# Bank assignment and order in the front of an attention + two-MoE kernel, and the place of one batch's sums of v

## The chip, the cores and the metric

One core of a Trainium2 chip. The time is the device time of one execution, in microseconds, as the median of several runs; lower is better. Before the change it is 967.26 us (three runs, 966.04 to 967.92).

## What is computed

```python
def _attn_ref(q, k, v):                    # 4 batches, 8 heads, 576 tokens, 64 wide
    q_d, k_d, v_d = means over 4 tokens    # 144 down-sampled tokens
    out_up = np.repeat(sm_attn(q_d, k_d, v_d), 4, axis=2)
    scores = scale * np.matmul(q, k.transpose(0, 1, 3, 2))
    scores = np.where(abs(i - j) < 4, scores, -1e9)      # a band of 7
    return out_up + softmax(scores) @ v
...
    x = attn.reshape(2304, 512)            # tokens of all batches
    x = (silu(x @ w_gate) * (x @ w_val)) @ w_out         # 512 -> 1536 -> 512
    h = x @ w_in                                         # 512 -> 2048
    return (h * clip(h + 3, 0, 6) / 6) @ w_out2          # -> 512
```

The weights arrive as 64-bit floating-point numbers. All results are float32.

## The kernel before

**The main loop** (from L1050) goes through five blocks of 8, 6, 8, 8 and 6 groups of 64 tokens, at most 512 tokens each. A block has 68 units, 36 for the first MoE layer (kinds G, V and O) and 32 for the second (H and P); a unit is 12 matmuls (the last two O or P units of a block are done together). Both operands are split into a high and a low part, so three products stand for one. `prefetch(i)` (L240) loads the raw weights of unit i + 8 on SyncE's queue, and converts and splits those of nearer units on ScalarE and VectorE. Beside the units of a block, VectorE works on the banded attention of a later batch, and TensorE on its down-sampled attention (`down_main`, L850; one job a unit from unit 36 on).

**The front** (`first_batch`, L317) prepares batch 0 on TensorE, ahead of unit 0:
- `load_T` (L436) transposes q and k, two heads (one index c of four) at a time: for each half two filler matmuls that keep TensorE at work, three transposes, and an evacuation by VectorE (q) or ScalarE (k).
- `sums(c)` adds groups of four tokens; `down_scores(c)` (L473), `down_trans(c)` (L502) and `down_values(c)` (L513) are the down-sampled attention of two heads: scores, maximum, four exponentials; norm, transposes, copies; values. The values read `vd`, which `load_vd` (L366) loads in four pieces through two buffers and adds up on GpSimd.
- The banded attention runs over five tiles of 122 query tokens: `scores(i)` (L528; the band as a matmul, 16 products, two maxima, 8 exponentials), `norm(i)`, `trans(i)` (L580), `values(i)` (L594). Values add the down-sampled result and leave the two parts of x in `xr`.
- Unit 0 is done in two column halves, 244 and 268 wide (L33 `HALVES`), so that its first half needs tiles 0 and 1 alone.

**PSUM** has 8 banks by tag: mm (two), acc0 to acc3, pa, px. In the front, `load_T` goes around acc0, acc1 and acc2; `down_scores` uses mm; scores(i) use acc0 and acc1 for even tiles and mm for odd ones; trans use acc2 and acc3; `down_values` acc3; `down_trans` and `values` pa and px.

**What sets the order.** A compile-time scheduler orders each engine's instructions by readiness and program order, and each engine then runs its queue in that order. `keep_in_program_order` (in `together`, `fill`, `late` and `behind`) pins an instruction behind the one traced just before it on its engine. In the front the fills, the transposes of `load_T`, the scores, `down_scores` and `down_values` are pinned; the other transposes and `values` are not. The order of calls is written out by hand (L635 to L678).

**Sums of later batches.** `down_sums(b, ...)` (L279) is a generator: for each of four tokens in a group it issues two GpSimd DMAs (halves of 72 groups) for q and k, then for v, the later three adding to what lies in SBUF. Each `next` gives one operand's pair. For batch 1 the 12 steps are spread over the front; for batches 2 and 3 they go along with a block, behind a gate: a one-element GpSimd copy that reads the last block's output tile (L280 to L282).

Of the kernel before, what the change touches and what calls it, by code (L numbers as in the profile page):

```python
# [10 lines left out]
F32 = mybir.dt.float32  # L11
# [24 lines left out]

VAL0 = {1: 2}
EXP_AT = 26

EARLY = 6  # L40

# [4 lines left out]
def tile_kernel(  # L46
# [12 lines left out]
    nc = tc.nc  # L59

    B, H, S, D = q.shape
    DM = H * D
# [3 lines left out]
    NJ = S // 4  # L66
    NJH = NJ // 2
    W = 7
    NC = DM // P
# [7 lines left out]
    UMAX = max(BLOCKS)  # L77
# [10 lines left out]
    def bank(tag, name, bufs=1):  # L88
        return pp.tile([P, 512], F32, tag=tag, name=name, bufs=bufs)
# [186 lines left out]

    dn, qk = {}, {}

    def down_sums(b, dn, qk):  # L279
        if b > 1:  # L280
            done = state["os"]
            tc.keep_in_program_order(nc.gpsimd.tensor_copy(consts[:, 60:61], done[:, (UMAX // 2 - 2) * DM:][:, :1]))  # L282
        for ws in ("qk", "v"):
            for t in range(4):
                for w in ws:
                    if t == 0:
                        dn[w] = sp.tile([NJH, 2, H, D], F32, tag="dn" + w, name=f"dn{w}{b}", bufs=1)
                    src = {"q": q, "k": k, "v": v}[w]
                    for half in range(2):
                        tok = src[b, :, half * NJH * 4:(half + 1) * NJH * 4, :].rearrange("h (j t) d -> j t h d", t=4)  # L290
                        how = {"accum_op": ALU.add} if t else {}
                        tc.keep_in_program_order(nc.gpsimd.dma_start(dn[w][:, half], tok[:, t], **how))
                    yield
# [23 lines left out]
    def first_batch():  # L317
# [6 lines left out]
        with tc.tile_pool(name="fp", bufs=1) as fp:  # L324
# [111 lines left out]
            def load_T(w, c):  # L436
                src = qn[w, c // 2]
                for th in range(2):
                    tag = ("acc0", "acc1", "acc2")[turn[0] % 3]
                    turn[0] += 1  # L440
                    ps = bank(tag, f"fT{w}{c}{th}")
                    fill(ps, 2)
                    ps = ps[:, :S // 2]
                    for t in range(3):
                        tc.keep_in_program_order(nc.tensor.transpose(
                            ps[:, t * TT:(t + 1) * TT],
                            src[:, 3 * th + t, c % 2 * 2:c % 2 * 2 + 2].rearrange("j h d -> j (h d)"),
                            ident[:TT, :TT],
                        ))
                    if w == "q":  # L450
                        nc.vector.tensor_scalar(
                            qT[:, c, th * S // 2:(th + 1) * S // 2], ps, 0.125, None, op0=ALU.mult
                        )
                    else:
                        nc.scalar.activation(kT[:, c, 3 + th * S // 2:3 + (th + 1) * S // 2], ps, AF.Copy)

            def sums(c):

                nc.vector.tensor_reduce(
                    qs[:, c], qT[:, c].rearrange("p (j t) -> p j t", t=4), axis=AX.X, op=ALU.add  # L460
                )
                nc.scalar.activation(ds[:, c], qs[:, c], AF.Copy, scale=1 / 16)
                nc.vector.tensor_reduce(
                    dk[:, c], kT[:, c, 3:S + 3].rearrange("p (j t) -> p j t", t=4), axis=AX.X, op=ALU.add
                )
# [7 lines left out]
            def down_scores(c):  # L473

                pss = []
                for par in range(2):
                    ps = bank("mm", f"fdS{2 * c + par}", 2)
                    if par:
                        fill(ps, 1)
                    pss.append(ps[:NJH, :2 * NJ].rearrange("p (g j) -> p g j", g=2))  # L480
                for half in range(2):
                    for par in range(2):
                        rows = slice(par * D, par * D + D)
                        together(nc.tensor.matmul(
                            pss[par][:, half], ds[rows, c, half * NJH:(half + 1) * NJH], dk[rows, c, :],
                            start=True, stop=True,
                        ))
                nm = fp.tile([NJH, 2, 2], F32, tag="fdnm", name=f"fdnm{c}", bufs=4)
                pd = fp.tile([NJH, 2, 2, NJ], F32, tag="fdpd", name=f"fdpd{c}", bufs=4)
                sd = fp.tile([NJH, 2, 2], F32, tag="fdsd", name=f"fdsd{c}", bufs=4)  # L490
                for par in range(2):
                    nc.vector.tensor_reduce(nm[:, par], pss[par], axis=AX.X, op=ALU.max, negate=True)
                    for half in range(2):
                        nc.scalar.activation(
                            pd[:, par, half], pss[par][:, half], AF.Exp, bias=nm[:, par, half:half + 1],
                            accum_out=sd[:, par, half:half + 1],
                        )
                dst[c] = pd, sd
# [12 lines left out]
                    nc.scalar.activation(dpt[h], pt, AF.Copy)  # L511

            def down_values(c):  # L513
                po = bank("acc3", f"fdO{c}")[:, :NJ]
                for kh in range(2):
                    for par in range(2):
                        together(nc.tensor.matmul(
                            po[par * D:par * D + D], vd[:, kh, 2 * c + par, :], dpt[2 * c + par][:, kh, :],
                            start=kh == 0, stop=kh == 1,
                        ))  # L520
                nc.vector.tensor_copy(od[:, c], po)
# [110 lines left out]
                    put_cols(bi, t0 + a - starts[bi] * UT, xf[:, :, a:e])  # L632
                    a = e

            ahead = down_sums(1, dn, qk)  # L635
            for c in range(NC):
                load_T("q", c)
                load_T("k", c)
                if c == NC - 1:
                    scores(0)  # L640
                if c:
                    down_scores(c - 1)
                sums(c)
                if c == 2:
                    prefetch(3 - LR)
                if c >= 2:
                    down_trans(c - 2)
            down_values(0)
            down_scores(3)
            next(ahead)  # L650
            scores(1)
            prefetch(4 - LR)
            norm(0)
            down_trans(2)
            down_values(1)
            next(ahead)
            trans(0)
            down_trans(3)
            down_values(2)
            scores(2)  # L660
            prefetch(5 - LR)
            norm(1)
            down_values(3)
            values(0)
            for i in range(1, NT):
                next(ahead, None)
# [368 lines left out]
    for bi in range(NB):  # L1035
# [30 lines left out]
        if db:  # L1066
            sums = down_T(db, dn, qk)
            if bi:
                sums = chain(down_sums(db, dn, qk), sums)
        for i in range(bi * NU, (bi + 1) * NU):  # L1070
            m = i - bi * NU
            prefetch(i)
# [19 lines left out]
            next(main, None)  # L1092
            if m == NU - EARLY:
                load_ahead(at + 1)
            step_x(limit)
            next_tick()
        if bi + 1 < NB:
# [37 lines left out]
```

## Time and profile before

| | |
|---|---|
| median of 3 runs | 967.26 us |
| the profiled execution: device time, span | 962.81 us, 961.0 us |
| busy: TensorE, its weight loads | 934.2 us, 789.1 us |
| busy: VectorE, ScalarE, GpSimd | 733.5 us, 506.7 us, 111.0 us |
| mean granted TensorE clock | 0.990 of full speed |
| moved by DMA | 160.79 MB |

PE is TensorE's matmuls, PEld its weight loads, DVE VectorE, ACT ScalarE, POOL GpSimd, SP SyncE; a queue issuing DMAs has a q behind its name. Matmul ends are modelled, so neighbouring ones can overlap by some tenths of a microsecond. Tiles carry the program's names: fT is the bank of `load_T`, fdS, fdT and fdO those of `down_scores`, `down_trans` and `down_values`, fS, fPT and fO those of the five tiles' scores, transposes and values; held are the exponentials, turned the transposed ones, vd and fvd the pieces and sums of batch 0's v, dnq, dnk and dnv the sums of later batches, pO the down-sampled values of these.

### The profile page before, as it was taken

How to read it: one execution, taken by the hardware profiler on the slowest of the kernel's cores; microseconds unless marked ns; L12 is line 12 of the kernel's file. 1: busy time of each engine (PE TensorE's matmuls, PEld its weight loads, DVE VectorE, ACT ScalarE, POOL GpSimd, SP SyncE). 2: the span in 40 equal slices, each digit the busy share in tenths (PEclk: the TensorE clock that was granted, in tenths of full speed). 3: DMA queues.
4: the chain of work that ended last, by engine and by line, in shares of the span. 5: the costliest groups of instructions: out<-in, count | busy, mean ns of one | idle time of the engine just before them, and what ended most of it. 6: DMA issues, size and time to landing. Idle time of an engine off the chain costs nothing.

```text
span 961.0 us, 12930 instructions
## 1 busy us (share of the span) xinstructions
PE 934.2 (97%) x4800; PEld 789.1 (82%) x4800; DVE 733.5 (76%) x1067; ACT 506.7 (53%) x945; POOL 111.0 (12%) x115
## 2 busy tenths in 40 slices
PE   8779999999999999999999999999999999999997
PEld 5567888777799988878888778888888888999996
DVE  7689967799889979999664799996347994445652
ACT  4676667876554577543244764443335444444542
POOL 5742000000053300015410000000000000000000
PEclk9789999999999999999999999999999999999999
DMA  8999999466699823359962212462323223434331
GB/s 207 170 271 316 327 341 351 155 209 226 238 287 270 176 72 108 123 189 237 203 139 96 78 66 85 160 216 90 108 88 105 92 88 112 152 132 132 119 123 33
DMA packets 116339, 160.79 MB, mean 167 GB/s; under 512 B 61868, under 2 KB 83756, under 8 KB 116276
## 3 DMA queue, kind: packets, MB, share of 16 engines
q1 hardware_dynamic: 67892, 131.41, 42.3%
q0 software_dynamic: 43488, 10.72, 11.1%
q10 hardware_dynamic: 4896, 17.83, 4.7%
q8 instruction: 38, 0.62, 0.3%
q14 instruction: 25, 0.20, 0.1%
HBM read 137.29 MB, written 22.54 MB: 166 GB/s over the span
## 4 chain that ended last, share of the span: by engine, by line
PE 83%; DVE 11%; ACT 3%; issue 2%; DMA 1%; SPq 0%; ACTq 0%; DVEq 0%
PE pH L938 17%; PE aP L980 16%; PE pG L938 15%; PE aO L980 15%; PE pV L938 15%; DVE wr L237 2%; DVE pv L809 1%; ACT held L560 1%; PE pS L863 1%; DVE xf L838 1%; DVE h L954 1%; PE pO L713 1%; DMA k<-in_k_dram 1%; DVE pv L813 1%; PE pPT L706 1%
## 5 line engine op out<-in xcount | busy, mean ns | idle before, releaser
L237 DVE TENSOR_TENSOR wr<-w,wr 128x1024 fp32r<-128x1024 f32 x170 | 207.5, 1221 | 121.6 <-ACT wr L236 121.3
L236 ACT ACTIVATE wr<-w 128x1024 fp32r<-128x1024 f32 x170 | 179.7, 1057 | 132.4 <-issue 63.1
L938 PE MATMUL pH<-x,wr 128*128 128x512 f32 (+1 forms) x960 | 212.4, 372 | 0.0
L980 PE MATMUL aP<-wr,gH 128*128 128x512 f32 x864 | 211.4, 395 | 0.3 <-ACT gH L955 0.3
L938 PEld LDWEIGHTS pH<-x,wr 128*128 128x128 f32 x960 | 173.0, 188 | 25.1 <-issue 2.5
L980 PEld LDWEIGHTS aP<-wr,gH 128*128 128x128 f32 x864 | 159.6, 188 | 35.1 <-issue 2.7
L938 PE MATMUL pG<-xr,wr 128*128 128x512 f32 (+3 forms) x732 | 156.5, 368 | 3.8 <-ACT xr L273 3.2
L938 PE MATMUL pV<-xr,wr 128*128 128x512 f32 (+1 forms) x720 | 153.4, 368 | 0.0
L980 PE MATMUL aO<-gV,wr 128*128 128x512 f32 (+1 forms) x720 | 152.7, 368 | 0.0
L938 PEld LDWEIGHTS pG<-xr,wr 128*128 128x128 f32 x732 | 133.4, 190 | 21.4 <-ACT xr L273 3.8
L938 PEld LDWEIGHTS pV<-xr,wr 128*128 128x128 f32 x720 | 130.9, 188 | 16.7
L980 PEld LDWEIGHTS aO<-gV,wr 128*128 128x128 f32 x720 | 130.8, 188 | 16.7
L953 ACT ACTIVATE h<-pH,consts 128x512 f32<-128x512 f32 (+1 forms) x80 | 51.5, 644 | 59.7 <-PE pH L938 59.4
L944 ACT ACTIVATE sl<-pG 128x512 f32<-128x512 f32 (+1 forms) x60 | 33.3, 556 | 72.9 <-PE pG L938 72.8
L955 ACT ACTIVATE gV<-sl 128x512 fp32r<-128x512 f32 (+1 forms) x60 | 35.0, 583 | 65.6 <-DVE sl L950 65.5
L955 ACT ACTIVATE gH<-h 128x512 fp32r<-128x512 f32 (+1 forms) x80 | 46.9, 586 | 32.1 <-DVE h L954 31.8
L954 DVE SCALAR_TENSOR_TENSOR h<-h,pH 128x512 f32<-128x512 f32 (+1 forms) x80 | 50.5, 631 | 14.8 <-ACT h L953 14.2
L772 DVE TENSOR_TENSOR pr<-q,k 128x1792 f32<-128x1792 f32 x27 | 54.5, 2020 | 8.3 <-DMA k<-in_k_dram 8.1
L956 DVE TENSOR_TENSOR gH<-h,gH 128x512 fp32r<-128x512 f32 (+1 forms) x80 | 50.5, 632 | 10.4 <-ACT gH L955 10.0
L214 ACT ACTIVATE top<-w 128x512 f16<-128x512 bf16 x68 | 52.1, 788 | 11.0 <-DMA w<-in_moe_w_out_dram 2.9
L809 DVE TENSOR_TENSOR pv<-sc,v 128x1792 f32<-128x1792 f32 x27 | 54.6, 2022 | 0.5
L775 DVE TENSOR_REDUCE sc<-pr 128x28 f32<-128x1792 f32 x27 | 54.3, 2013 | 0.2
(125 smaller groups left out, 758.4 us busy)
## 6 DMA issues: line engine op xcount, KB each, us to landing
w<-kept SPq DMA_DIRECT2D x136, 512.0 KB
kept<-w ACTq DMA_DIRECT2D x34, 512.0 KB
w<-in_moe_w_out_dram SPq DMA_DIRECT2D x28, 512.0 KB
w<-in_moe_w_in_dram SPq DMA_DIRECT2D x16, 512.0 KB
w<-in_moe_w_gate_dram SPq DMA_DIRECT2D x12, 512.0 KB
w<-in_moe_w_val_dram SPq DMA_DIRECT2D x12, 512.0 KB
out_dram<-os SPq DMA_DIRECT2D x16, 256.0 KB
dnq<-in_q_dram POOLq DMA_DIRECT2D x24, 144.0 KB, 7.4
```

The lines of the kernel that those rows point to most:

```text
L214: behind(nc.scalar.activation(halves(top[i % 2], 2, F16)[:, :, 1], h3.bitcast(BF16), AF.Copy))
L236: behind(nc.scalar.activation(r[:, :, 0], s, AF.Copy))
L237: behind(nc.vector.tensor_tensor(r[:, :, 1], s, r[:, :, 0].bitcast(F32), op=ALU.subtract))
L772: nc.vector.tensor_tensor(pr, qt[:, a:a + SUB, None, :].to_broadcast([P, SUB, W, D]), win(kt, a, SUB), op=ALU.mult)
L775: nc.vector.tensor_reduce(sc[:, a:a + SUB], pr, axis=AX.X, op=ALU.add)
L809: nc.vector.tensor_tensor(pr, pe[:, a:a + SUB, :, None].to_broadcast([P, SUB, W, D]), win(vt, a, SUB), op=ALU.mult)
L938: nc.tensor.matmul(ps[:, cs], r[:, a, c], x[:, c, b_, cs], start=part is HIGH and a == c == 0, stop=part is LOW and c == NC - 1,)
L953: nc.scalar.activation(h, ps, AF.Relu, scale=1 / 6, bias=half1[:, 0:1])
L954: nc.vector.scalar_tensor_tensor(h, h, 1.0, ps, op0=ALU.min, op1=ALU.mult)
L955: nc.scalar.activation(g[:, 0, :nt], h, AF.Copy)
L956: nc.vector.tensor_tensor(g[:, 1, :nt], h, g[:, 0, :nt].bitcast(F32), op=ALU.subtract)
L980: nc.tensor.matmul(ps, **one, start=f_ == 0 and a == b_ == 0, stop=f_ == nf - 1 and b_ == 1,)
```

## The change

Three things: banks, order, and the sums of v of batch 1.
- `load_T` goes around acc0, acc1 and both mm banks; `down_scores` uses acc2 and acc3; `down_values` uses pa.
- `down_values(c - 2)` follows `down_trans(c - 2)` inside the loop over c. scores(1) follows `sums(3)`, right behind `down_scores(2)`. `norm(0)` stands ahead of `down_scores(3)`, and `down_values(3)` ahead of scores(2).
- In the front the generator gives q and k alone (8 steps). The four steps of v are issued in one go once unit 31 of the first block has been traced, behind a gate that reads the first element of the latest gated product g. For batches 2 and 3 the gate is the same as before, handed in as an argument.

```diff
+SUMV = 31
...
-    def down_sums(b, dn, qk):
-        if b > 1:
-            done = state["os"]
-            tc.keep_in_program_order(nc.gpsimd.tensor_copy(consts[:, 60:61], done[:, (UMAX // 2 - 2) * DM:][:, :1]))
-        for ws in ("qk", "v"):
+    def down_sums(b, kinds, gate=None):
+        if gate is not None:
+            tc.keep_in_program_order(nc.gpsimd.tensor_copy(consts[:, 60:61], gate))
+        for ws in kinds:
...
-                    tag = ("acc0", "acc1", "acc2")[turn[0] % 3]
+                    tag = ("acc0", "acc1", "mm", "mm")[turn[0] % 4]
                     turn[0] += 1
-                    ps = bank(tag, f"fT{w}{c}{th}")
+                    ps = bank(tag, f"fT{w}{c}{th}", 2 if tag == "mm" else 1)
...
-                    ps = bank("mm", f"fdS{2 * c + par}", 2)
+                    ps = bank(f"acc{2 + par}", f"fdS{2 * c + par}")
...
-                po = bank("acc3", f"fdO{c}")[:, :NJ]
+                po = bank("pa", f"fdO{c}")[:, :NJ]
...
-            ahead = down_sums(1, dn, qk)
+            ahead = down_sums(1, ["qk"])
             for c in range(NC):
                 load_T("q", c)
                 load_T("k", c)
...
                 if c:
                     down_scores(c - 1)
                 sums(c)
+                if c == NC - 1:
+                    scores(1)
                 if c == 2:
                     prefetch(3 - LR)
                 if c >= 2:
                     down_trans(c - 2)
-            down_values(0)
+                    down_values(c - 2)
+            norm(0)
             down_scores(3)
             next(ahead)
-            scores(1)
             prefetch(4 - LR)
-            norm(0)
             down_trans(2)
-            down_values(1)
+            down_values(2)
             next(ahead)
             trans(0)
+            norm(1)
             down_trans(3)
-            down_values(2)
+            down_values(3)
             scores(2)
             prefetch(5 - LR)
-            norm(1)
-            down_values(3)
             values(0)
...
-                sums = chain(down_sums(db, dn, qk), sums)
+                sums = chain(down_sums(db, ["qk", "v"], state["os"][:, (UMAX // 2 - 2) * DM:][:, :1]), sums)
...
+            if i == SUMV:
+                last = [t for key, t in state.items() if key[0] == "g"][-1]
+                for _ in down_sums(1, ["v"], last[:, 0, :1].bitcast(F32)):
+                    pass
             step_x(limit)
```

## Rows read from the trace of the kernel before

**Rows 1.** The page, busy time of each engine with its share of the span.
```profile
PE 934.2 (97%) x4800; PEld 789.1 (82%) x4800; DVE 733.5 (76%) x1067; ACT 506.7 (53%) x945; POOL 111.0 (12%) x115
```
**Rows 2.** Busy time by stretch, the sum over the first 80 us.
```profile
sum 80.00, PE 64.29 PEld 47.54 DVE 59.67 ACT 49.69 POOL 44.61; mean PE 1.61 PEld 1.19 DVE 1.49 ACT 1.24 POOL 1.12
```
**Rows 3.** The chain of waits in order of time: start us, us, engine and work.
```profile
23.02 2.25 ACT held L560 x13
```
**Rows 4.** TensorE in order of time from 16.4 us: start us, us, instruction.
```profile
16.50 0.69 PE L706 MATMUL fdT<-ident,fdpd 72*72 72x72 f32 x8 [0.71 <-DVE fdpd L506]
17.03 0.60 PE L434 MATMUL fTq<-idle 128*128 128x512 bf16 x2
...
19.51 0.41 PE L445 MATMUL fTk<-ident,fnk 96*128 96x96 f32 x3
20.77 0.64 PE L544 MATMUL fS<-band,pick 64*122 64x512 bf16 x4 [0.85 <-ACT fkT L455]
...
23.81 0.71 PE L517 MATMUL fdO<-fdpT,fvd 72*64 72x144 f32 x8
```
**Rows 5.** GpSimd in order of time, the second piece of v and its last addition.
```profile
19.75 1.26 POOL L375 TENSOR_TENSOR vd<-vd 72x512 f32<-72x512 f32 x1 [3.92 <-DMA vd<-in_v_dram]
21.09 1.12 POOL L376 TENSOR_TENSOR fvd<-vd 72x256 f32<-72x256 f32 x1
```
**Rows 6.** ScalarE in order of time, with the idle time ahead in brackets.
```profile
30.57 0.38 ACT L494 ACTIVATE fdpd<-fdS,fdnm 72x144 f32<-72x144 f32 x1 [2.01 <-DVE fdnm L492]
...
32.01 0.70 ACT L511 ACTIVATE fdpT<-fdT 72x288 f32<-72x288 f32 x2
34.06 0.58 ACT L592 ACTIVATE turned<-fPT 128x488 f32<-128x488 f32 x1 [1.35 <-PE fPT L588]
37.81 0.58 ACT L592 ACTIVATE turned<-fPT 128x488 f32<-128x488 f32 x1 [3.17 <-PE fPT L588]
```
**Rows 7.** Stretches: us, each engine's busy time (instructions), granted clock, DMA share, GB/s.
```profile
24.40:28.00 3.60, 1.10 (x11) 0.55 (x9) 2.28 (x5) 3.60 (x20) 1.13 (x1) 0.99 0.79 177
28.00:38.00 10.00, 8.48 (x50) 6.12 (x49) 5.13 (x11) 3.47 (x15) 9.36 (x10) 0.50 0.66 185
23.02:65.25 42.23, 29.87 (x286) 23.04 (x283) 31.46 (x61) 32.18 (x128) 27.20 (x23) 0.84 1.03 190
```
**Rows 8.** VectorE in order of time, from the first step of `down_trans` to its product.
```profile
15.09 0.16 DVE L504 TENSOR_SCALAR fdsd<-fdsd 72x4 f32<-72x4 f32 x1
...
15.49 0.95 DVE L506 TENSOR_TENSOR fdpd<-fdpd,fdsd 72x576 f32<-72x576 f32 x1
```
**Rows 9.** VectorE and TensorE in order of time, around 70 and 77 us.
```profile
69.64 2.03 DVE L772 TENSOR_TENSOR pr<-q,k 128x1792 f32<-128x1792 f32 x1 [2.10 <-DMA k<-in_k_dram]
...
77.51 5.76 PE L938 MATMUL pG<-xr,wr 128*128 128x512 f32 x24 [0.60 <-DVE sl L950]
```
**Rows 10.** The tile dnv's time to landing, then GpSimd in order of time.
```profile
DMA to landing us min/median/max: 4.5/7.0/13.6
...
56.20 2.83 POOL L292 DMA_DIRECT2D dnv<-in_v_dram  x2
...
90.45 2.89 POOL L292 DMA_DIRECT2D dnv<-in_v_dram  x2 [9.62 <-DMA dnv<-in_v_dram]
266.46 1.77 POOL L282 COPY consts<-os 128x1 f32<-128x1 f32 x1 [173.12 <-ACT os L1005]
...
301.25 2.83 POOL L292 DMA_DIRECT2D dnv<-in_v_dram  x2
...
326.20 2.77 POOL L292 DMA_DIRECT2D dnv<-in_v_dram  x2 [3.93 <-DMA dnv<-in_v_dram]
```
**Rows 11.** ScalarE and TensorE in order of time, and one stretch (columns as in rows 7).
```profile
156.60 0.61 ACT L955 ACTIVATE gV<-sl 128x512 fp32r<-128x512 f32 x1
...
185.86 0.72 PE L713 MATMUL pO<-pT,dnv 72*64 72x144 f32 x8
...
175.00:180.00 5.00, 5.00 (x30) 3.72 (x31) 2.87 (x9) 4.79 (x16) 0.00 (x0) 1.00 0.05 17
```

## The prediction

> **What bounds the kernel now.** I read the page first, then the stretches, then the chain of waits, then each engine's order of time over the first 66 us. TensorE is busy for 97% of the span [rows 1]. Over the first 80 us it is busy for 64.29 us [rows 2], so 15.7 of its 26.8 idle microseconds (961.0 less 934.2) lie there, in the front that prepares batch 0, and the rest is scattered. Behind the front TensorE runs without a break, so the end of the kernel moves with the time at which the last columns of batch 0 are ready (xr, about 65.3 us), and with any wait that TensorE meets after that. In the front the chain goes back and forth between engines: VectorE takes the maxima of tile 0's scores, and from 23.02 us ScalarE takes their exponentials [rows 3]. From there to 65.25 us ScalarE works 32.18 of 42.23 us [rows 7]. So a change to the front can win or lose in two ways: the time at which these 32 us of work start, and the 10.05 us of holes in them.
>
> The sum is made on the profiled execution, 962.81 us around a span of 961.0; the median of the three runs is 967.26, so 4.45 is added at the end. A measurement of this kernel can tell about 0.2% from no change, 1.9 us.
>
> **Part by part. 1, down-sampled values brought forward.** `down_values(0)` used to stand behind `down_scores(2)`, and TensorE ran it at 23.81 us, right after other work [rows 4]. Now it stands in the pass c = 2, ahead of `load_T` of the last pair of heads; its matmuls, and the fills and transposes of `load_T`, are all pinned behind what was traced before them on TensorE, so nothing can pass it. It needs the sums of v of heads 0 to 3. GpSimd makes these: it waited for the second load of v until 19.75, and finished the last addition that heads 0 and 1 need at 21.09 + 1.12 = 22.21 us [rows 5]. The order of the loads and of GpSimd's work before that does not change. So TensorE, which began `load_T` at 17.03 [rows 4], stands in front of `down_values(0)` until 22.21; that takes 0.71 [rows 4], and `load_T` begins at 22.92, **5.9 us later**. Queued behind the wait are the 24 matmuls of `load_T` (to 19.92 before, 2.89 us), tile 0's scores, which need all of them, and through these ScalarE's exponentials: 23.02 becomes 28.9. ScalarE and VectorE have only the exponentials and the norm of `down_scores(1)` to do meanwhile, and did those in the same place before.
>
> **2, the clock.** Before, TensorE was busy 1.10 of 3.60 us from 24.4 to 28.0, and then ran ten microseconds at a granted clock of 0.50, the 1.2 GHz level [rows 7]. The new wait is longer (from the end of the transposes at 17.2 to 22.2), so I expect such a stretch behind it. If everything from the start of `load_T` to the first exponential (17.03 to 23.02) took twice its time, it would cost 6.0 us; if the clock does not fall, nothing. I take 1.4, half of the 2.89 of `load_T`, as the rest of that stretch is waits and work of other engines.
>
> **3, two tiles' scores in a row.** ScalarE's three longest holes before are 2.01 us for the maxima of `down_scores(3)`, then 1.35 and 3.17 for the two halves of tile 0's transposes [rows 6]. They arise because scores(1) used the banks of `down_scores(3)` and came only after its exponentials, so ScalarE had nothing of tile 1 to do. With scores(1) straight behind scores(0), tile 1's exponentials lie there (of tile 0's 16 instructions 13 took 2.25 us [rows 3]), and all three holes, 6.53 us, can close. A new one opens: scores(2) is now pinned behind `down_values(3)` rather than `down_values(2)`. From the last exponential of `down_scores(3)` to the first of tile 2 there are two small VectorE steps and the product (15.09 to 16.44, 1.35) [rows 8], the transposes and the values of a pair of heads (0.69 and 0.71; both in [rows 4]), ScalarE's copy between them, 0.70 [rows 6], and tile 2's scores with the first maximum, for which tile 0's stand (20.77 to 23.02, 2.25 [rows 3, 4]): 1.35 + 0.69 + 0.70 + 0.71 + 2.25 = 5.7. ScalarE has the copies of tile 0's transposes (two of 0.58), one more 0.70 and a weight conversion in it, some 3.2 us, so the new hole is 2.5. Holes: 6.5 - 2.5 = **4.0 us won**. The other 3.5 us (two waits for maxima, one at the end) I leave. Bounds: all 10.05 closed, or none.
>
> **4, banks of their own.** `load_T` over four banks instead of three: no gain, its matmuls ran without a wait before [rows 4]. `down_scores` on acc2 and acc3: the third still waits for the exponentials of the second, only on other banks; and trans(0), on the same two, now waits for the exponentials of `down_scores(3)`, which is counted in 3. `down_values` on pa, shared with one half of the down-sampled transposes: one small VectorE copy between two pairs, beside ScalarE's work. These go at nothing; were ScalarE not busy, each would cost less than ScalarE's own copy, 0.70 [rows 6].
>
> **5, the sums of v leave the front.** Eight GpSimd transfers of 144 KB, in four rounds (each adds to what the round before landed; two halves a round, 1.4 us of GpSimd each), were issued from 56.20 to 93.3 us [rows 10]. Nothing waited for GpSimd there. What they shared was the DMA engines: VectorE stood 2.10 us for the first chunk of k at 69.64, and through it TensorE 0.60 us at 77.51 [rows 9]. I take **0.6 us won**; the least is nothing.
>
> **6, the sums of v behind unit 31.** What is added is one GpSimd copy as a gate, reading the last gated product (unit 31's, ready at 156.60 + 0.61 = 157.2 [rows 11]), 1.77 us [rows 10], and the same eight issues on GpSimd's queue, which holds nothing else until 266.46. SyncE's queue is not passed. TensorE needs the sums at 185.86 [rows 11], where the first down-sampled values of batch 1 stand in its order. From 159.0 on four rounds are needed. Bounds: at the shortest landing, 4.5 us [rows 10], four rounds and the second half's issue are 19.4 us, 178.4, no wait; at batch 1's own pace (34.25 us to the last round's issue, then 1.4 and 7.0) they end at 201.7, a wait of 15.8. Between: batch 2 took 24.95 us to the issue of its last round, 8.3 a round. Here the DMA engines are nearly idle from 175 to 180 (0.05 [rows 11]), so I take two rounds at 8.3 and two at 4.5 with 1.4 behind them: 159.0 + 16.6 + 9.0 + 1.4 = 186.0. That is the time of the need, and I take **no wait**; what covers it is TensorE's own work from 157 to 185.86, and it is just enough.
>
> The Trainium skill ("DMA: Bandwidth & Descriptors", the section on the anatomy of one DMA) fits one such transfer as 2.0 us plus its bytes over 436 GB/s, an estimate of 2.3 us here, so that four rounds would be through by about 170 and no wait possible. This trace has 4.5 us at the least and 7.0 as median for the same transfers; the measurement decides, by the page the rival of late sums below would have no chance, and the sum would stay as it is.
>
> Sum: 5.9 + 1.4 - 4.0 - 0.6 = **+2.7 us**. 962.81 + 2.7 = 965.5 for a profiled execution, 970.0 for the median.
>
> **The rivals.** *The order wins after all* (faster): the late start is paid, but ScalarE then works almost without holes. It would end at 28.9 + 32.2 = 61.1 with none, 4.2 us ahead of before, 4.8 with the chunk of k: 962.5. It decides when under about 2 us of holes are left, that is, when the clock does not fall and scores(2) and scores(3) come early enough to follow each other too. For it: 6.5 of 10.05 us have one cause, which goes. Against it: all the waits of 3. At 1 to 2 us of holes it is 963.5 to 964.5. *The sums of v are late* (slower): at batch 2's pace (24.95 + 1.4 + 7.0 = 33.4 from 159.0) they end at 192.4, and TensorE stands 6.5 us at 185.9: 970.0 + 6.5 = 976.5; at batch 1's pace 985.8. For it: both batches worked out here took over 33 us. Against it: the DMA engines are nearly idle from 175 on. *Nothing net*: the 5.9 us are paid in full by holes that close (6.5 and no new one of weight), 967; this is also what would be seen if the compile-time order of the unpinned VectorE and ScalarE work changes little beyond the pins.
>
> **How the numbers follow.** The forecast has 0.40, of which about 0.08 falls within 0.2%; the faster rival 0.28; late sums of v 0.18; nothing net 0.14, of which 0.03 lies above the bound. Faster 0.28; same 0.08 + 0.11 = 0.19; slower 0.32 + 0.18 + 0.03 = 0.53. The range runs from the faster rival with no holes, 962.5, to late sums at batch 2's pace, 977; beyond lie the pace of batch 1 and a front in which no hole closes and the clock costs its 6.0 us (967.26 + 5.9 + 6.0 = 979). The likeliest case alone: 967 to 973.
>
> **What would show it.** Step 1: a gap on TensorE before `down_values(0)` that ends with GpSimd's addition, about 22.2; `load_T` from 22.9; the first exponentials of the tiles at 28 to 31. If `load_T` still starts near 17, step 1 is wrong and the change is faster by 4 us or more. Step 2: a granted clock of 0.5 after that gap. Step 3: ScalarE's holes from the first exponential to the last xr down from 10 to about 6 us, the longest one ahead of tile 2. Step 5: no 0.6 us gap near 77. Step 6: TensorE's first down-sampled values of batch 1 without a wait of more than 1 to 2 us.

## The result, and the profile after

The changed kernel takes **975.16 us** as the median of four runs (973.14 to 976.55), the kernel before 966.65 us beside it (four runs, 965.94 to 967.92): a ratio of 1.0085 [1.0063, 1.0107], **8.5 us slower**. The profiled execution of the changed kernel is one of 975.35 us with a span of 973.6; that of before (962.81) was a short one for its kernel, so the two traces are 12.5 us apart, where the medians are 8.5. Line numbers after are one higher up to the generator (L273 is L274) and the same from there through the front.

The page after, busy time as in [rows 1], then the sum over the first 80 us as in [rows 2]:

```profile
PE 941.1 (97%) x4798; PEld 793.2 (81%) x4800; DVE 732.2 (75%) x1067; ACT 506.4 (52%) x945; POOL 109.9 (11%) x116
```
```profile
sum 80.00, PE 60.65 PEld 44.15 DVE 49.63 ACT 44.81 POOL 36.65; mean PE 1.52 PEld 1.10 DVE 1.24 ACT 1.12 POOL 0.92
```

In the first 80 us TensorE does 3.6 us less than before. Over the span it is busy 6.9 us longer, at a mean granted clock of 0.982 instead of 0.990: more of its work ran at the lower level. TensorE in order of time, changed kernel, as in [rows 4]; the last row is the second half of unit 0, which was at 65.09 before:

```profile
17.75 0.69 PE L706 MATMUL fdT<-ident,fdpd 72*72 72x72 f32 x8 [1.00 <-DVE fdpd L506]
21.92 0.67 PE L706 MATMUL fdT<-ident,fdpd 72*72 72x72 f32 x4 [3.47 <-DVE fdpd L506]
22.52 1.23 PE L517 MATMUL fdO<-fdpT,fvd 72*64 72x144 f32 x8
24.07 0.63 PE L434 MATMUL fTq<-idle 128*128 128x512 bf16 x1 [0.33 <-issue]
...
37.56 1.52 PE L517 MATMUL fdO<-fdpT,fvd 72*64 72x144 f32 x8 [5.55 <-ACT fdpT L511]
...
44.01 1.34 PE L517 MATMUL fdO<-fdpT,fvd 72*64 72x144 f32 x8
...
47.81 1.23 PE L517 MATMUL fdO<-fdpT,fvd 72*64 72x144 f32 x8
48.97 1.11 PE L544 MATMUL fS<-band,pick 64*122 64x512 bf16 x4
...
73.73 6.07 PE L938 MATMUL pG<-xr,wr 128*128 128x268 f32 x24
```

TensorE stands ahead of `down_values(0)` (22.52) as forecast, and `load_T` begins at 24.07 instead of 17.03. The wait is recorded at the row before: four of the transposes of heads 2 and 3, which are not pinned, had come ahead of the values. The fdO rows are the four pairs of heads; tile 2's scores (48.97) stand behind the last of them. GpSimd's last addition for heads 0 and 1, as in [rows 5], ended at 20.44 + 0.72 = 21.16:

```profile
20.44 0.72 POOL L376 TENSOR_TENSOR fvd<-vd 72x256 f32<-72x256 f32 x1
```

ScalarE in order of time, changed kernel, as in [rows 3, 6]; the rows named held are the first exponential of tiles 0, 2 and 4:

```profile
30.12 0.37 ACT L560 ACTIVATE held<-fS,fnm 122x128 f32<-122x128 f32 x1 [1.66 <-DVE fnm L558]
...
37.05 0.76 ACT L511 ACTIVATE fdpT<-fdT 72x288 f32<-72x288 f32 x2
41.31 0.38 ACT L494 ACTIVATE fdpd<-fdS,fdnm 72x144 f32<-72x144 f32 x1 [3.50 <-DVE fdnm L492]
...
46.96 0.70 ACT L511 ACTIVATE fdpT<-fdT 72x288 f32<-72x288 f32 x2 [1.96 <-PE fdT L706]
...
51.90 0.37 ACT L560 ACTIVATE held<-fS,fnm 122x128 f32<-122x128 f32 x1 [3.78 <-DVE fnm L558]
...
64.48 0.34 ACT L560 ACTIVATE held<-fS,fnm 88x94 f32<-88x94 f32 x1 [1.98 <-DVE fnm L558]
```

The two holes at tile 0's transposes [rows 6] are gone, but the one ahead of the exponentials of `down_scores(3)` is 3.50 now (2.01 before), and holes of 1.96, 3.78 and 1.98 have come. From the first exponential to the last xr they add up to 12.2 us, with two small ones of 0.20 and 0.76; before it was 10.05.

Stretches, changed kernel (columns as in [rows 7]): behind the first wait, behind the second, and from the first exponential to unit 0's second half.

```profile
20.00:26.00 6.00, 3.75 (x20) 2.58 (x22) 2.13 (x5) 1.38 (x4) 1.08 (x2) 0.50 0.98 242
...
38.00:50.00 12.00, 11.70 (x70) 8.50 (x70) 4.52 (x10) 4.86 (x16) 8.45 (x7) 0.50 1.18 129
30.12:73.73 43.61, 30.31 (x273) 23.61 (x270) 29.16 (x59) 31.43 (x126) 21.64 (x18) 0.77 0.88 159
```

After each of the two waits (3.47 and 5.55 us) TensorE works at a granted clock of 0.50, the 1.2 GHz level; in the second of these stretches it is busy 11.70 of 12 us, so there the half clock itself sets the pace.

Behind the front, changed kernel: VectorE and TensorE at the chunk of k (as in [rows 9]), GpSimd's sums of v (as in [rows 10]), and TensorE's down-sampled values of batch 1 (as in [rows 11]):

```profile
78.25 2.03 DVE L772 TENSOR_TENSOR pr<-q,k 128x1792 f32<-128x1792 f32 x1 [2.06 <-DMA k<-in_k_dram]
```
```profile
86.12 5.75 PE L938 MATMUL pG<-xr,wr 128*128 128x512 f32 x24 [0.55 <-DVE sl L950]
...
196.84 0.71 PE L713 MATMUL pO<-pT,dnv 72*64 72x144 f32 x6 [1.43 <-DMA dnv<-in_v_dram]
...
264.55 0.41 PE L829 MATMUL px<-ident,o 128*128 128x128 f32 x2 [2.26 <-DVE o L815]
```
```profile
164.95 0.83 POOL L282 COPY consts<-gV 128x1 f32<-128x1 f32 x1 [109.30 <-ACT gV L955]
...
190.42 2.77 POOL L292 DMA_DIRECT2D dnv<-in_v_dram  x2 [3.54 <-DMA dnv<-in_v_dram]
```

The wait for the chunk of k is what it was, 0.55 against 0.60, and a wait of 1.43 for the sums of v has come.

### The profile page after: what moved, and what is told of

Read it like the earlier page. It is cut to its first block, busy times and chain, and to the rows that moved or that the text cites. A ratio compares the mean times of both kernels' runs of the same rounds, so it can differ in the third digit from the quotient of the medians.

```text
span 973.6 us, 12929 instructions
## 1 busy us (share of the span) xinstructions
PE 941.1 (97%) x4798; PEld 793.2 (81%) x4800; DVE 732.2 (75%) x1067; ACT 506.4 (52%) x945; POOL 109.9 (11%) x116
## 4 chain that ended last, share of the span: by engine, by line
PE 69%; issue 14%; DVE 6%; DMA 4%; POOL 3%; SPq 2%; ACT 1%; ACTq 0%; POOLq 0%; DVEq 0%
PE aP L980 16%; PE pH L938 16%; PE pG L938 11%; PE pV L938 11%; PE aO L980 11%; DVE wr L238 2%; SPq L131 1%; DMA dnv<-in_v_dram 1%; DMA vd<-in_v_dram 1%; DMA dnq<-in_q_dram 1%; DVE pv L809 1%; PE pO L713 1%; POOL dnq L292 1%; PE pS L863 1%; DVE xf L838 1%
## 5 line engine op out<-in xcount | busy, mean ns | idle before, releaser
L955 ACT ACTIVATE gH<-h 128x512 fp32r<-128x512 f32 (+1 forms) x80 | 46.9, 586 | 31.9 <-DVE h L954 31.7
```

Of the source, the lines that this page charges most:

```text
L955: nc.scalar.activation(g[:, 0, :nt], h, AF.Copy)
```

## The experiments

In all runs three rows tell where a kernel stands: unit 0's second half, the first unit that waits for VectorE's sl (pG), and the wait for o (px) near 257 us. Each row is named by the tile that it writes. From px to the end every kernel here takes 709.1 to 712.7 us, so most of what differs between them is there by px, and 3.7 us are not. All times in us; the last two columns are the median and the ratio to the kernel before, run beside it.

| kernel | second half | pG [wait] | px | profiled run | median | ratio |
|---|---|---|---|---|---|---|
| before | 65.09 | 77.51 [0.60] | 253.75 | 962.81 | 966.65 | |
| r1, before again | 65.55 | 79.20 [1.82] | 256.96 | 968.94 | 968.78 | 1.0014 [0.9994, 1.0034] |
| changed | 73.73 | 86.12 [0.55] | 264.55 | 975.35 | 975.16 | 1.0085 [1.0063, 1.0107] |
| r2, v in front | 75.24 | 89.33 [3.80] | 267.04 | 977.83 | 977.39 | 1.0094 [1.0062, 1.0126] |
| r3, v alone | 65.89 | 78.62 [1.21] | 255.96 | 967.81 | 968.49 | 1.0014 [0.9992, 1.0036] |
| r4, values late | 70.55 | 83.40 [2.59] | 263.25 | 973.19 | 972.12 | 1.0041 [1.0020, 1.0062] |
| r5, banks alone | 68.83 | 80.48 [0.75] | 256.70 | 967.64 | 967.08 | 0.9990 [0.9971, 1.0009] |
| r6, fills | 72.56 | 85.31 [2.46] | 266.72 | 977.06 | 977.06 | 1.0084 [1.0051, 1.0117] |
| r7, tile 1 behind | 72.13 | 84.72 [2.31] | 263.39 | 973.34 | 976.30 | 1.0098 [1.0061, 1.0136] |
| r8, r4 and tile 1 | 68.91 | 81.82 [2.63] | 261.99 | 973.42 | 971.83 | 1.0038 [1.0016, 1.0059] |
| r9, tile 2 ahead | 72.67 | 84.75 [0.60] | 262.12 | 973.09 | 974.30 | 1.0075 [1.0054, 1.0097] |
| r10, tile 2 up | 68.66 | 80.59 [0.35] | 257.89 | 970.63 | 971.13 | 1.0042 [1.0022, 1.0063] |
| r11, r8, tile 2 up, unit 25 | 64.45 | 77.42 [1.17] | 258.94 | 970.12 | 969.65 | 1.0014 [0.9993, 1.0036] |
| r12, r11 at unit 31 | 62.31 | 77.31 [3.51] | 257.04 | 966.26 | 967.32 | 1.0008 [0.9984, 1.0032] |

### What repeats, and what each of the three parts does alone

**r1**, the kernel before, unchanged.

> The kernel before once more, for a second profile of it. The two profiles shown differ by 12.5 us (962.81 and 975.35), the medians by 8.5 (966.65 and 975.16). Theory: the first profiled execution of before was a short one, so a second one lies near the median, 966 to 967, with the front as long as in the first (the last columns of unit 0 start at 65 us, within 0.5) and the other 3 to 4 us lost behind the front. Rival: the front itself varies by microseconds from run to run, and then the second profile's front is longer by 2 us or more.

The front repeats within 0.9 us here: `load_T` at 17.87 and tile 0's exponentials at 23.93 are 0.8 and 0.9 later than in the first trace, the second half 0.5. What follows repeats less: pG is 1.7 later (it waits 1.82 instead of 0.60), px 3.2, the end 6.1. The profiled execution (968.94) and the median (968.78) both lie above the 966 to 967 expected. r11 and r12 below, whose fronts are the same, differ by 2.1 us at the second half; so a difference of 1 to 2 us between two traces says little.

**r2**, the changed kernel with the sums of v in the front again.

```diff
-SUMV = 31
+SUMV = -1
...
-            ahead = down_sums(1, ["qk"])
+            ahead = down_sums(1, ["qk", "v"])
```

> The changed kernel with batch 1's sums of v back in the front; banks and order stay changed. Theory (the order of the front costs 8.6 us, the place of v's sums about 2): the wait of 1.43 us before the down-sampled values of batch 1 goes, the median is 973 to 974, that is 1.5 to 2 below 975.2, and still 6.5 us above before. Rival 1 (v's sums are the main cost): 968 or less. Rival 2 (v's sums cost nothing net, because the chunk of k lands earlier without them): 975 or more.

The wait for the sums of v is gone and the median is no lower (rival 2). TensorE's wait at pG is 3.80 here: the time is only lost elsewhere. **r3** is the opposite, the kernel before with nothing but the sums of v moved behind unit 31.

> The kernel before with only the sums of v moved behind unit 31; banks and order as before. Theory: the same wait appears at TensorE, some 1.5 us, and the 0.6 us wait near 77 us stays: 968 to 969. Rival (the move wins its 0.6 us and waits for nothing): 966. Rival (late sums at the pace of batch 2): 973.

No difference from no change: 0.60 us of wait for the sums of v, and none gained at k (1.21). Step 5's gain is not there and step 6's cost is under what the median can tell.

**r5**, the kernel before with the changed banks, order and sums of v untouched (the three `bank` lines of the diff).

> The kernel before with the new banks alone: its order of calls, and its sums of v in the front. Theory (the order costs, the banks by themselves do not): scores(1) no longer waits for the exponentials of down_scores(3), so it runs some 5 us earlier than at 35 us, the two holes of 1.35 and 3.17 us ahead of tile 0's copies shrink, the last columns of unit 0 start at 62 to 65 us, and the median is 964 to 967.5. Rival (the shared banks acc2, acc3 and pa are what costs): 970 or more.

No change in the median, but the expectation for the front (shorter holes, second half at 62 to 65) missed. The banks let tile 1's scores come 3.5 us earlier (31.56 instead of 35.04). Yet `down_values(0)`, which ran in acc3 at 23.81 without a wait [rows 4], now stands 4.16 us for ScalarE's copies. Its own operands were there by 21.2; its new bank, pa, holds transposes of head 2 until ScalarE has copied them, behind tile 0's exponentials. `down_scores(3)` is pinned behind it, and the hole ahead of its exponentials is 3.48 (2.01 before). TensorE, then ScalarE, r5:

```profile
27.98 1.23 PE L517 MATMUL fdO<-fdpT,fvd 72*64 72x144 f32 x8 [4.16 <-ACT fdpT L511]
```
```profile
32.28 0.38 ACT L494 ACTIVATE fdpd<-fdS,fdnm 72x144 f32<-72x144 f32 x1 [3.48 <-DVE fdnm L492]
```

The hole ahead of tile 2 grows to 5.07 (1.36 before). The second half starts 3.3 behind that of r1, but its 24 matmuls take 5.13 us instead of the 6.06 of before, VectorE waits less for k, and pG follows only 1.3 behind that of r1. By the medians neither r3 nor r5 loses anything, and r2, with the sums of v in the front, loses as much as the changed kernel: what costs is the new **order** on these banks. The new order on the old banks was not run.

### The late start

**r4**, the changed kernel with `down_values(0)` and (1) behind the loop.

```diff
                 if c >= 2:
                     down_trans(c - 2)
-                    down_values(c - 2)
+            down_values(0)
+            down_values(1)
```

> The changed kernel with down_values(0) and (1) called behind the loop over c, so that load_T of the last heads is not held by the sums of v; scores(1) stays straight behind scores(0). Theory (the late start, 7.1 us, passes to the end in full): load_T starts at 17 to 18.5, the first exponentials at 24 to 25, and the median is 968 to 970. Rival 1 (ScalarE's holes take the gain, since down_scores(3) still waits for copies that stand behind tile 1's exponentials): 972 or more.

`load_T` begins at 18.26 and tile 0's exponentials at 23.50, 6.6 us ahead of the changed kernel, but the second half comes only 3.2 ahead, and the median is 972.12. ScalarE in order of time, r4, shows where the other half stays:

```profile
37.66 0.38 ACT L494 ACTIVATE fdpd<-fdS,fdnm 72x144 f32<-72x144 f32 x1 [5.09 <-DVE fdnm L492]
...
48.72 0.37 ACT L560 ACTIVATE held<-fS,fnm 122x128 f32<-122x128 f32 x1 [4.25 <-DVE fnm L558]
```

The holes of 3.50 and 3.78 have become 5.09 and 4.25. TensorE, r4, before the first of them:

```profile
32.42 1.23 PE L517 MATMUL fdO<-fdpT,fvd 72*64 72x144 f32 x8 [6.92 <-ACT fdpT L511]
```

It stands 6.92 us for ScalarE's copies of heads 2 and 3, which are queued behind both tiles' exponentials. (`down_values(0)` needs them for its bank, as in r5, and `down_values(1)` right behind it as operands.) `down_scores(3)`, which is to feed ScalarE next, is pinned behind these values. **So the two tiles in a row feed ScalarE first and starve it afterwards.**

**r6**, 16 fillers ahead of `down_values(0)`, to keep TensorE at work in the wait.

```diff
-                po = bank("pa", f"fdO{c}")[:, :NJ]
+                po = bank("pa", f"fdO{c}")
+                if c == 0:
+                    fill(po, 16)
+                po = po[:, :NJ]
```

> The changed kernel with 16 filler matmuls (3.4 us) traced ahead of down_values(0), so that TensorE is at work while the sums of v are made. Theory of the clock: the granted clock stays at 1.0 through load_T and tile 0's scores, load_T takes 2.9 us again instead of 3.8, and the median falls by about 1, to 974. Rival (the fillers end after the sums are ready, or the time is taken back by ScalarE): 975 to 977.

Stretches, r6:

```profile
17.00:22.00 5.00, 4.36 (x30) 2.18 (x27) 3.42 (x7) 2.51 (x11) 1.98 (x2) 1.00 1.00 296
22.00:28.00 6.00, 6.00 (x58) 4.07 (x58) 3.17 (x6) 1.82 (x4) 1.50 (x2) 1.00 0.91 214
```

The clock stays at 1.00, and tile 0's exponentials start at 28.29 instead of 30.12: the clock behind this wait costs about 1.8 us at that place. It is worth 1.2 at the second half, and nothing that the median shows: 977.06, at the upper end of the rival's 975 to 977 (waits of 2.46 for sl and 2.10 for the sums of v).

### The holes

**r7**, the changed kernel with scores(1) moved behind `down_trans(1)`, so that the copies of heads 2 and 3 come ahead of tile 1's exponentials.

```diff
-                if c == NC - 1:
-                    scores(1)
                 if c == 2:
                     prefetch(3 - LR)
                 if c >= 2:
                     down_trans(c - 2)
+                if c == NC - 1:
+                    scores(1)
+                if c >= 2:
                     down_values(c - 2)
```

> The changed kernel with scores(1) called behind down_trans(1), so that ScalarE's copies of the down-sampled transposes of heads 2 and 3 stand ahead of tile 1's exponentials. Theory (TensorE stood 5.55 us for these copies at 37.56, and down_scores(3), the hole of 3.50 us and a stretch at half clock follow from it): down_values(1) runs at about 34, the hole goes, and the median is 971 to 973. Rival (the hole only moves to the next wait, and the front's end is set elsewhere): 975.

It does what it is for: TensorE's wait falls from 5.55 to 2.63, the hole of 3.50 goes. The second half starts only 1.6 earlier, and the median is the same as the changed kernel's within its spread (four runs, 973.34 to 980.13). ScalarE, r7, shows where part of the gain goes: the next hole is longer.

```profile
50.22 0.37 ACT L560 ACTIVATE held<-fS,fnm 122x128 f32<-122x128 f32 x1 [4.42 <-DVE fnm L558]
```

**r8** joins both: the values of heads 0 to 3 behind the loop, scores(1) between them.

```diff
-                if c == NC - 1:
-                    scores(1)
...
-                    down_values(c - 2)
+            down_values(0)
+            scores(1)
+            down_values(1)
```

> Both repairs at once: down_values(0) behind the loop, the copies of down_trans(1) ahead of tile 1's exponentials, and scores(1) between down_values(0) and (1). Theory: the late start and the hole of 3.5 to 5 us both go, and the median is 967 to 969.5, that is 3 to 5 below the run with down_values(0) late alone. Rival (holes behind down_scores(3) remain whatever comes before): 971 or more.

It gives 4.8 us at the second half, and a median of 971.83, no better than r4 alone. The hole ahead of tile 2 is 4.42 again, and there is one of 3.91 ahead of tile 1: scores(1) is pinned behind `down_values(0)`, which waits 4.17 us for its bank as in r5. TensorE, then ScalarE, r8:

```profile
28.36 1.23 PE L517 MATMUL fdO<-fdpT,fvd 72*64 72x144 f32 x8 [4.17 <-ACT fdpT L511]
```
```profile
33.10 0.37 ACT L560 ACTIVATE held<-fS,fnm 122x128 f32<-122x128 f32 x1 [3.91 <-DVE fnm L558]
```

`down_values` back on acc3 in this order was not tried.

**r9** puts scores(2) ahead of `down_values(3)` again, where the kernel before has it, in the changed kernel.

```diff
-            down_values(3)
             scores(2)
             prefetch(5 - LR)
+            down_values(3)
```

> The changed kernel with one line moved: scores(2) stands ahead of down_values(3) again, as in the kernel before (there it was at 39.65, in the changed kernel at 49.87, behind the values of heads 6 and 7 at 47.81). Everything else is the changed kernel's, the late start of 7 us and the waiting sums of v included. Theory (the pin behind down_values(3) makes the hole of 3.8 us ahead of tile 2): tile 2's scores come by 47.5, the hole ahead of tile 2's exponentials is under 2 us, unit 0's second half starts at 70.5 to 71.8 instead of 73.73, and the median is 971.5 to 974. Rival (the holes are ScalarE's wait for VectorE and for a TensorE at half clock, whatever the order: what closes here opens elsewhere): tile 2's exponentials come earlier, but the second half starts within 1 us of 73.73 and the median is 974.5 or more.

The hole falls only to 2.30, one of 1.35 opens at tile 1's transposes, and the second half comes 1.1 earlier: between the two expectations, nearer the rival. In this trace the pin behind one pair's values is worth about 1 us, no more than two traces of one front can differ by. **r10** takes scores(2) out of the down-sampled chain altogether: it follows `down_scores(3)`.

```diff
             prefetch(4 - LR)
+            scores(2)
             down_trans(2)
...
             down_values(3)
-            scores(2)
             prefetch(5 - LR)
```

> The changed kernel with scores(2) traced straight behind down_scores(3), ahead of the down-sampled transposes of heads 4 and 5: a third tile in the row, which acc0 and acc1 allow as soon as tile 0's exponentials are done (34.0 in the changed kernel). Late start and sums of v as in the changed kernel. Theory (the holes of 3.50 ahead of the exponentials of down_scores(3) and 3.78 ahead of tile 2 are gaps of order): the hole ahead of tile 2 is gone, the one of 3.50 stays, the second half of unit 0 starts at 69.5 to 71.5, the median is 970 to 973.5. Rival (the holes only move, here ahead of tile 0's transposes and the down-sampled ones, which now stand behind eight more exponentials): second half at 73 or later, median 974.5 or more.

ScalarE in order of time, r10, the rows with idle time ahead, behind the first exponential and up to the last xr:

```profile
41.72 0.38 ACT L494 ACTIVATE fdpd<-fdS,fdnm 72x144 f32<-72x144 f32 x1 [3.50 <-DVE fdnm L492]
...
44.46 0.70 ACT L511 ACTIVATE fdpT<-fdT 72x288 f32<-72x288 f32 x2 [0.52 <-PE fdT L706]
...
53.80 0.61 ACT L274 ACTIVATE xr<-fxf 128x488 fp32r<-128x488 f32 x1 [1.51 <-DVE fxf L625]
...
68.15 0.59 ACT L274 ACTIVATE xr<-fxf 128x96 fp32r<-128x96 f32 x2 [0.76 <-DVE fxf L619]
```

They sum to 6.3 us instead of 12.2; the second half is 5.1 earlier (even a little more than the theory asked), and the median 4 us lower than the changed kernel's. From the first exponential (30.53) to the second half 38.13 us pass, where 42.07 passed before: 3.9 won, which is what the forecast had put down for the holes, 4.0. The late start is still in it, and the median lies 4.0 above the 967.09 of the kernel before beside it.

### All of it together

**r11** has r8's order, scores(2) as in r10, and the gate of the sums of v at unit 25 (`SUMV = 25`).

> Three repairs of the changed kernel together: down_values(0) and (1) behind the loop with scores(1) between them (second half at 68.91 with these alone), scores(2) straight behind down_scores(3), and the gate of the sums of v at unit 25 instead of 31, some 19 us earlier. Theory (the late start, the hole ahead of tile 2 and the wait of 1.4 to 2.1 us for the sums of v are the whole of the loss, and each comes off by itself): second half at 65 to 67, no wait of TensorE for dnv over 0.3 us, median 965 to 968.5, level with the kernel before or below it. Rival (what is won at the front or at the sums of v is given back behind, or the holes move): second half at 68 or later, median 970 or more. At unit 25 the transfers may also fall among others and slow the block's own; then TensorE waits for a load between 140 and 180 that the changed kernel does not have.

The front is now ahead of the kernel before by 0.6, and there is no wait for the sums of v. But their transfers, 140 to 177 us, fall among the loads of weights. ScalarE's waits over the whole run, r11, then TensorE in order of time:

```profile
ACT top L215 <- DMA w<-in_moe_w_in_dram: 9.7, 4, 3.1
```
```profile
168.44 3.02 PE L938 MATMUL pH<-x,wr 128*128 128x512 f32 x11 [2.54 <-ACT x L993]
...
176.09 3.01 PE L938 MATMUL pH<-x,wr 128*128 128x512 f32 x12 [1.26 <-DVE h L954]
```

That is 3.8 us of TensorE, more than the 1.43 that was to be saved. That the transfers make these waits is likely, but not shown: 9.7 us is twice the longest of the other thirteen traces, but these have anything from nothing to the 4.7 of r5, which has no transfers of v there. The median, 969.65, lies between the two expectations. **r12** is the same with the gate back at unit 31.

> The kernel of r11_late_s2_v25 with the gate of the sums of v back at unit 31; nothing else differs. There the eight transfers, from 140 to 177 us, fell among the loads of weights of the first block: ScalarE stood 9.7 us for them and TensorE 2.54 and 1.26 us for ScalarE and VectorE around 168 and 176, while the front had come 0.6 us ahead of the kernel before (64.45). Theory (that wait is the price of unit 25, and the front's gain lasts): ScalarE waits for the same load under 3 us, TensorE has no wait over 0.5 us between 150 and 180, it waits 1 to 2.2 us for dnv as the other kernels with unit 31, second half at 64 to 65.5, profiled execution 964 to 967 and median 966 to 968.5, level with the kernel before. Rival (something else behind the front takes the time, for instance the clock after the wait around 260): median 969.5 or more.

ScalarE waits 4.6 us for the same loads (the expectation was under 3), TensorE 0.61 at the place of the 1.26, and under 0.3 for the sums of v. The medians of r11 and r12 cannot be told apart (1.0014 and 1.0008, with intervals that overlap); the place of the gate rests on the traces. r12's median is 967.32, level with the kernel before: **with the values of heads 0 to 3 late, scores(1) between them and scores(2) up, the whole of the loss is gone.** Alone, the late values (r4) are 3.0 and scores(2) up (r10) 4.0 us below the changed kernel; the place of scores(1) gave nothing beside r4 (r8). r4 and r10 joined without it were not run. The second half, 62.31, is even 2.8 us ahead of before; the row of pG shows that this is not kept, and its 24 matmuls take 7.36 us, against 5.76 before (TensorE, r12):

```profile
77.31 7.36 PE L938 MATMUL pG<-xr,wr 128*128 128x512 f32 x24 [3.51 <-DVE sl L950]
```

The chunk of k is issued as the front ends, and VectorE's work on it stands ahead of what TensorE needs. SyncE's issues of k, before and in r12 (count, duration, first and last start), with VectorE's first product in r12:

```profile
L130 SPq DMA_DIRECT2D k<-in_k_dram x14: 257/426/516, 62.0 to 631.5; - x14
```
```profile
L131 SPq DMA_DIRECT2D k<-in_k_dram x14: 236/440/818, 59.1 to 635.0; - x14
```
```profile
69.44 2.02 DVE L772 TENSOR_TENSOR pr<-q,k 128x1792 f32<-128x1792 f32 x1 [4.84 <-DMA k<-in_k_dram]
```

Issued 2.9 us earlier, it is there at 69.44 instead of 69.64 [rows 9]. In all fourteen traces pG starts 7.86 or 7.87 us after VectorE's first product on k, so this landing and not the end of the front sets pG. No kernel here had its pG before 77.3; whether an earlier chunk would keep the front's gain was not tried.

## Why the prediction was right in sign, and short in size

The forecast was 970.0 us with a range of 962.5 to 977; measured were 975.16. The range and the sign held, the likeliest case (967 to 973) did not.

**Steps 1 and 2 held.** The sum had 5.9 for the start of `load_T` and 1.4 for the clock, 7.3 at the first exponential. Measured: 30.12 - 23.02 = 7.10. The place and the fall of the clock are as forecast; r4 (start undone) and r6 (clock kept) show both. The end of the gap is not quite: GpSimd's addition was there at 21.16, and what ended the gap at 21.92, 0.8 us behind it, is VectorE's product for the half of `down_trans(1)` that had slipped ahead of the values. Against r1 the start is 6.2 later rather than 7.0. (`load_T` has 20 matmuls, not 24; nothing rests on that.)

**Step 3 failed**, the "4.0 us won" at ScalarE's holes. From the first exponential to the second half 43.61 us pass where 42.07 passed before (the 42.23 of [rows 7] ends 0.16 later): 1.5 lost. ScalarE had 0.6 us less to do there (31.43 against 32.02) and 2.1 more of holes. The difference to the sum is 5.5 us, and the whole forecast missed by 8.5 - 2.7 = 5.8. Two things in that step were wrong. It let "all three holes, 6.53 us" close, and looked at scores(1) only as work for ScalarE; it did not follow what is queued behind it: eight exponentials ahead of the copies of heads 2 and 3, TensorE's wait of 5.55 for these, and `down_scores(3)` pinned behind. That hole grew from 2.01 to 3.50 (r7: gone once the copies go first). And it priced the way from the last exponential of `down_scores(3)` to the first of tile 2 mostly by durations at the full clock, 5.7 us, less 3.2 of ScalarE's work (of which some 1.3 stands for a weight conversion that no row there gives): a hole of 2.5. TensorE was at half clock for 12 us there, behind the wait of 5.55, and also ran tile 0's transposes; the way took 9.15 (42.75 to 51.90), with 3.4 of work and holes of 1.96 and 3.78. The faster rival named the right condition, scores(2) early enough: r10 meets it and gains 5.1 us at the second half, but keeps 6.3 us of holes where the rival allowed 2. The measured time lies near the rival of late sums of v (976.5), yet these cost 1.43 of it: the range held for another reason than the one that set its upper part.

**Step 4** put the banks at nothing. The median of r5 bears that out, the mechanism does not: for pa it saw only a small VectorE copy, and r5 has a wait of 4.16 us for ScalarE's copies and a second half 3.3 us behind that of r1. **Step 5** (0.6 won) fell: the wait is 0.55, and r3 has 1.21 without the sums of v. What set it is the time at which k is issued, 7.6 us ahead of its use in both traces. **Step 6** (no wait) missed by 1.43 in this execution, by nothing (r7) to 2.1 in the others with unit 31; r3's median cannot tell its 0.60 from no change. The four rounds took 196.84 - 164.95 = 31.9 us from the gate; the estimate had 28.8. By the estimate from the figure of the Trainium skill ("DMA: Bandwidth & Descriptors", the anatomy of one DMA), 2.3 us a transfer, there would have been no wait; the runs speak against it here.

From the changed kernel's trace to that of before it is 12.5 us, to r1's 6.4; the median's 8.5 lies between, and the front's 8.6 is the part that the runs explain. Behind the front the traces show where executions differ. In the 4 us from px on the granted clock is 1.00 in before, r4, r6, r7 and r12, and 709.1 to 710.3 us follow to the end; it is 0.57 to 0.67 in the other nine, and 710.8 to 712.7 follow. Within each group the time grows, by and large, with TensorE's next wait for o, near 345 us, which is 0.35 to 1.71. What decides either stays open. So does this: r5 and r10 are within 0.2 us of each other at the second half and at pG and 1.2 apart at px, yet their medians are 4.1 apart (967.08 and 971.13). A row of the front tells the median only to some microseconds.

## What to carry to other kernels

When independent work is brought forward to fill an engine's holes, follow what it is queued ahead of on that engine, and what is pinned behind that on the others: here two tiles in a row cost the same engine its next input. Before a reader is moved up in a hand-written order, compare the time at which its operand is ready with the time at which everything queued behind it could have started. Ask the same of a bank: here sharing one tied values to copies that they do not read. And repairs that overlap must be joined before they are judged: r7 and r9 gave 1 to 2 us at the second half and r8 no lower median than r4, as each left the next hole open.

## What the runs showed of the hardware

- The same wait of TensorE (2.22 to 2.48 us at px in the fourteen traces) was followed by a granted clock of 1.00 in five and by a lower one in nine. Before and r2, with like waits for o later on (0.41 and 0.36), need 709.06 and 710.79 us from px to the end. Stretches of before, then of after, each behind that wait:

```profile
254.00:256.00 2.00, 2.00 (x11) 1.66 (x10) 1.73 (x5) 0.42 (x1) 0.00 (x0) 1.00 0.15 58
```
```profile
266.00:268.00 2.00, 2.00 (x6) 1.62 (x5) 1.97 (x5) 1.05 (x2) 0.00 (x0) 0.50 0.54 133
```

- A load's landing did not follow its issue closely: VectorE had the first chunk of k 7.3 us after its issue in r10 (65.39 to 72.72) and 10.3 in r12 (59.10 to 69.44), with the other traces between.
- A gap in GpSimd's work is no gap in the DMA engines: in the kernel before GpSimd did nothing from 150 to 175 us, and the DMA engines' mean busy share was 1.01 (columns as in [rows 7]):

```profile
150.00:175.00 25.00, 25.00 (x116) 19.99 (x115) 19.29 (x31) 19.19 (x34) 0.00 (x0) 1.00 1.01 351
```
